# Attention and longformer MLP: the order of a batch's attention inside the MLP groups, and the slots of loads, transposes and copies

## The chip, the cores and the metric

The kernel runs on one core of a Trainium2 chip. A core has a matrix engine (PE, TensorE), three engines for elementwise work (DVE or VectorE, ACT or ScalarE, POOL or GpSimd) and a queue that issues transfers (SP, SyncE). Each takes its instructions in the order in which they stand. The metric is the device time of one execution in microseconds; smaller is better.

## The reference

Eight batches of eight heads of attention over 576 positions of 64 values. A position sees those at most 32 away; eight global positions see all and are seen by all. The heads are put side by side (512 values a position) and go through a residual MLP that mixes the positions first and then the channels.

```
mask = np.abs(pos[:, None] - pos[None, :]) <= window
mask = mask | is_global[:, None] | is_global[None, :]
scores = np.where(mask, scale * np.matmul(q, k.transpose(0, 1, 3, 2)), -1000000000.0)
x = softmax(scores) @ v
...
a1 = alpha1 * x + beta1
u = x + lam * np.einsum('ts,bsd->btd', w_tok, a1)
a2 = alpha2 * u + beta2
out = u + lam * (np.maximum(a2 @ w_ch1, 0.0) @ w_ch2)
```

## The kernel before

**Attention of a batch.** Heads are taken in four pairs (hp). For a pair, `sc_unit` (three of them, u = 0, 1, 2) multiplies QP (the queries, padded and with the global queries behind each block) by KT into one of two PSUM banks, and ACT writes the exponentials E. After the third unit DVE makes PGQ (the global queries' share, L295) and PT (the masked band, L300). `gk_half` gives the scores of all queries against the global keys (EG, then G on DVE). `gq_pv` multiplies PGQ by V; ACT and then DVE (L315, L316) make RG of it, one of two buffers. `pv_x` and `pv_y` (five tiles, `pv_mms`) add G x RG and PT x V; DVE takes the reciprocal (L341) and norms into XR or SR (L348), and POOL multiplies by lambda alpha into XL (L366, L392, L396). The products of `gq_pv`, `pv_x`, `pv_y` and the token mix share a ring of three banks.

**Token mix.** `tok_tile` multiplies XL by the token weights; DVE adds it to XR (L405); POOL scales it into UB, one of two buffers (L420); SP issues a transposing transfer into UT (L421). UT, one of two buffers, is the MLP's input.

**MLP.** The 36 row tiles are taken in nine groups of four (GROUPS). A group is 128 matmuls of 128x512: 64 for the first layer (ACT's ReLU into HT, L488) and 64 for the second, whose result DVE scales and adds (L503, L504) and SP writes out (L507, L509). Group 1 takes the four tiles of batch 1; group 2 a shared tile of the batches 0 and 1 and the first three of batch 2; the later groups need fewer tiles of the batch just mixed.

**What sets the order.** All of it is written out by hand. The loop runs over the groups g = 0 to 8; the 128 matmuls are slots 0 to 127. `weave` spreads a list of atoms (a weight and a function) over a range of slots, in proportion to the weights: those of the attention of batch g + 1 (`attention`, or `first_attention` for batch 1 in group 0) and of its token mix. `timed` spreads by count: for batch g + 2 the loads on POOL (`prefetch`: K and Q in five chunks each, then V in five), on SP the transposes of K and Q into KT and QT (`xbars`) and a copy of V (`copy_vo`), and on DVE the copies from QT to QP (`qpad`, L210, eight of them) and of the global columns (`gcols`, L216 and L222). QP and QT have one buffer each; KT, V and its copy have two.

Of the kernel before, what the change touches and what calls it, by code (L numbers as in the profile page):

```python
# [20 lines left out]
HP = 4  # L21
# [65 lines left out]
def kernel(ctx, tc, q, k, v, global_idx, alpha1, beta1, w_tok, alpha2, beta2, w_ch1, w_ch2, lam, out):  # L87
# [160 lines left out]
    def gk_half(b, hf):  # L248
        def f():
            ps = sc_ps()  # L250
            qs = slice(288 * hf, 288 * hf + 288)
            for hp in range(HP):
                mm(ps[:, 0:288], KGP[:, hp, :], QT[:, hp, qs], hp == 0, hp == HP - 1)
            nc.scalar.activation(out=EG[:, qs], in_=ps[:, 0:288], func=AF.Exp, bias=0.0, scale=0.125)
            if hf == 1:
                g_rows()

        return (1.0, f)
# [14 lines left out]
    def sc_unit(b, hp, u):  # L273
        def f():
            ps = sc_ps()
            e = E[hp % 2]
            off = 0
            for t in (3 * u, 3 * u + 1, 3 * u + 2):
                n = 72 if t % 2 == 0 else 64
                mm(  # L280
                    ps[:, off : off + 2 * n].rearrange("p (a j) -> p a j", a=2),
                    KT[b % 2][:, hp, 64 * t : 64 * t + P],
                    QP[:, hp, :, t, 0:n],
                    True,
                    True,
                )
                off += 2 * n
            nc.scalar.activation(out=e[:, UOFF[u] : UOFF[u + 1]], in_=ps[:, 0:off], func=AF.Exp, bias=0.0, scale=0.125)  # L288
            if u == 2:
                pt, pg = PT[hp % 2], PGQ[hp]  # L290
                p0, p1 = pt.ap[0], e.ap[0]
                gq_in = bass.AP(e.tensor, e.offset + 64, [p1, [272, 5], [72, 2], [1, 8]])
                gq_m = bass.AP(gqm.tensor, gqm.offset, [gqm.ap[0], [8, 5], [0, 2], [1, 8]])
                for c0 in (64, 96):
                    nc.vector.tensor_tensor(  # L295
                        out=pg[:, :, c0 : c0 + 16].rearrange("p c (a g) -> p c a g", a=2), in0=gq_in, in1=gq_m, op=ALU.mult
                    )
                for par, n in ((0, 5), (1, 4)):
                    w = 72 if par == 0 else 64
                    nc.vector.tensor_tensor(  # L300
                        out=bass.AP(pt.tensor, pt.offset + 64 + 128 * par, [p0, [256, n], [1216, 2], [1, 64]]),
                        in0=bass.AP(e.tensor, e.offset + 144 * par, [p1, [272, n], [w, 2], [1, 64]]),
                        in1=bass.AP(mask.tensor, mask.offset + 64 * par, [mask.ap[0], [128, n], [0, 2], [1, 64]]),
                        op=ALU.mult,
                    )

        return (0.6, f)

    def gq_pv(b, hp):
        def f():  # L310
            ps = pv_ps()
            for c in range(5):
                mm(ps[:, 0:130], PGQ[hp][:, c, :], Ve[b % 2][:, c, 2 * hp : 2 * hp + 2, :].rearrange("p a e -> p (a e)"), c == 0, c == 4)
            rg = RG[hp % 2]
            nc.scalar.activation(out=rg, in_=ps[:, 0:130], func=AF.Copy, bias=0.0, scale=C32[:, 36:37])  # L315
            nc.vector.scalar_tensor_tensor(  # L316
                out=rg[96:128], in0=ps[96:128, 0:130], scalar=1.0 / GSC, in1=rg[96:128], op0=ALU.mult, op1=ALU.subtract
            )

        return (0.9, f)  # L320
# [29 lines left out]
    def xl_eng(b):  # L350
        return nc.gpsimd

    def pv_x(b, hp):
        st = {}

        def tile_i(i):
            def f():
                if i == 0:
                    st["ps"] = pv_ps()
                pv_mms(b, hp, i, st["ps"][:, 130 * i : 130 * i + 130])  # L360
                if i == 2:
                    base = 4 * (b % 3)
                    xo = XR[:, base : base + 3, 128 * hp : 128 * hp + 128]
                    norm(st["ps"], recip(st["ps"], 3), 0, 3, 0, P, xo.rearrange("p i (a d) -> p i a d", a=2))
                    l = LA1[:, 128 * hp : 128 * hp + 128]
                    xl_eng(b).tensor_tensor(  # L366
                        out=XL[b % 2][:, 0:3, 128 * hp : 128 * hp + 128],
                        in0=xo,
                        in1=bass.AP(l.tensor, l.offset, [l.ap[0], [0, 3], [1, 128]]),
                        op=ALU.mult,  # L370
                    )

            return (0.75, f)

        return [tile_i(i) for i in range(3)]

    def pv_y(b, hp):
        st = {}
        par = b % 2
        cs = slice(128 * hp, 128 * hp + 128)  # L380

        def f3():
            st["ps"] = pv_ps()
            pv_mms(b, hp, 3, st["ps"][:, 0:130])

        def f4():
            ps = st["ps"]
            pv_mms(b, hp, 4, ps[:, 130:260])
            xo = XR[:, 4 * (b % 3) + 3, cs]
            rt = recip(ps, 2)  # L390
            norm(ps, rt, 0, 1, 0, P, xo.rearrange("p (i a d) -> p i a d", i=1, a=2))
            xl_eng(b).tensor_tensor(out=XL[par][:, 3, cs], in0=xo, in1=LA1[:, cs], op=ALU.mult)  # L392
            r0 = 64 * par
            xo = SR[r0 : r0 + 64, (b // 2) % 2, cs]
            norm(ps, rt, 1, 1, r0, r0 + 64, xo.rearrange("p (i a d) -> p i a d", i=1, a=2))
            xl_eng(b).tensor_tensor(out=XL4[par][r0 : r0 + 64, cs], in0=xo, in1=LA1[r0 : r0 + 64, cs], op=ALU.mult)  # L396

        return [(0.75, f3), (0.4, f4)]
# [37 lines left out]
    def tok_shared(p):  # L436
# [15 lines left out]

        return [half(0), half(1)]

    def attention(b):
        a = []
        for i in range(HP + 1):
            s = [sc_unit(b, i, u) for u in range(3)] if i < HP else []
            w = pv_x(b, i - 1) + pv_y(b, i - 1) if i > 0 else []
            if i == 0:  # L460
                a += s + [gk_half(b, 0), gk_half(b, 1)]
            elif not s:
                a += w
            else:
                a += [s[0], s[1], w[0], w[1], w[2], s[2], w[3], w[4]]
            if i < HP:
                a.append(gq_pv(b, i))
        return a

    def token_mix(b):  # L470
        a = [tok_tile(b, i) for i in range(4)]
# [108 lines left out]
    def first_attention(b):  # L580

        pss = [None, None]

        def hold():
            pss[0], pss[1] = pv_ps(), pv_ps()

        def s(hp):
            return [sc_unit(b, hp, u) for u in range(3)]

        tail = s(0) + [gk_pair(0, pss)] + s(1) + [gk_pair(1, pss), gk_pair(2, pss), gk_pair(3, pss), gq_pv(b, 0)]  # L590
        if b == 0:
            a = [tr_pair(b, hp) for hp in range(HP)] + [(0.0, lambda: gcols(b)), (0.0, hold)] + tail
        else:
            a = [tr_pair(b, 0), (0.0, lambda: gcols(b)), (0.0, hold), tr_pair(b, 1)] + tail[0:4] + [tr_pair(b, 2)] + tail[4:8] + [tr_pair(b, 3)] + tail[8:]
        for hp in range(HP):
            s3 = s(hp + 2) if hp + 2 < HP else []
            g1 = [gq_pv(b, hp + 1)] if hp + 1 < HP else []
            a += s3[0:2] + pv_x(b, hp) + pv_y(b, hp) + g1 + s3[2:3]
        return a

    VF = [t.bitcast(FP32) for t in Vef]
# [230 lines left out]
    for g in range(9):  # L832
        base = mlp(g)
        slots = [[] for _ in range(129)]
        nb = g + 2
        if nb < NB:
            if nb % 2 == 0:
                pr = nb // 2
                slots[1].append(lambda pr=pr: gather(pr))
                slots[44] += [lambda: gather_x(0), lambda: gather_x(1)]  # L840
                slots[56].append(lambda pr=pr: gather_tr(pr, 0))
                slots[60].append(lambda pr=pr: gather_tr(pr, 1))
            timed(prefetch(nb), slots, 2, 60)
            timed(xbars(nb), slots, 60, 100)
            timed([lambda hp=hp: qpad(hp) for hp in range(HP)] + [lambda: gcols(nb)], slots, 116, 127)

        def wrap(i):
            def f():
                for s in slots[i]:
                    s()  # L850
                base[i]()

            return f

        items = [wrap(i) for i in range(128)]
        if g == 0:
            parts = [(first_attention(1), 4, 112), (token_mix(1), 112, 124)]
        elif g + 1 < NB:
            parts = [(attention(g + 1), 2, 90), (token_mix(g + 1), 94, 114)]
        else:  # L860
            parts = []
        weave(items, parts)
# [30 lines left out]
```

## Time and profile before

| | us |
|---|---|
| median of three runs | 435.84 |
| lowest and highest of them | 433.72, 438.39 |
| the profiled execution's own time | 438.8 |
| its span, first to last instruction | 437.0 |
| first matmul of the groups 0 to 8 | 55.3, 109.7, 152.1, 197.3, 240.3, 285.6, 328.6, 376.0, 403.6 |
| granted clock of PE, mean | 0.981 |

A row of the timeline gives the start and the length in us, the engine, the line in the code, the operation, the tile written and the tiles read, and in brackets how long the engine had been idle and what ended that. Rows of equal instructions are merged (x8). PEld is PE's weight load, SPq the queue of SP. A line of waits gives total, number and longest. A matmul's shown end is modelled.

### The profile page before, as it was taken

What the parts mean: (1) busy time and instruction counts of PE and PEld (TensorE: products, weight loads), DVE (VectorE), ACT (ScalarE), POOL (GpSimd) and SP (SyncE); (2) the same over time, 40 slices, a digit from 0 to 9 for tenths busy, and PEclk for the clock granted to TensorE, in tenths of its full rate; (3) what the DMA queues carried; (4) which work ended last, traced back from release to release, by engine and by line L of the source; (5) the groups of instructions that cost most, each with busy time, mean ns of one, the idle gap of its engine ahead of it and who ended that gap; (6) DMA issues with size and microseconds to landing.
All of it is one profiled execution on the core that took longest, in us unless ns stands there. A gap on an engine that the chain in (4) does not pass through costs nothing.

```text
span 437.0 us, 7829 instructions
## 1 busy us (share of the span) xinstructions
PE 383.1 (88%) x2925; PEld 210.3 (48%) x2977; DVE 236.4 (54%) x616; ACT 169.1 (39%) x315; POOL 212.0 (49%) x272
## 2 busy tenths in 40 slices
PE   2385799888999989998999899979997999999994
PEld 1264455543555455544554465445544554444442
DVE  4787464567355746655557565664566365304022
ACT  3563057400681078006820681057304830360720
POOL 8845962435693479347844793377441225100000
PEclk9999889999899999999999999999998999999998
DMA  8999999153994599469966994799673003201002
GB/s 205 206 218 251 221 181 141 11 145 74 126 127 69 133 147 147 57 137 137 141 68 146 138 146 65 125 134 150 67 149 64 1 1 84 72 1 72 26 24 73
DMA packets 162858, 48.97 MB, mean 112 GB/s; under 512 B 147642, under 2 KB 156674, under 8 KB 162820
## 3 DMA queue, kind: packets, MB, share of 16 engines
q0 software_dynamic: 98848, 16.92, 56.1%
q1 hardware_dynamic: 63172, 31.15, 34.5%
q8 instruction: 23, 0.38, 0.4%
q10 hardware_dynamic: 800, 0.39, 0.4%
q14 instruction: 15, 0.12, 0.1%
HBM read 39.34 MB, written 9.44 MB: 112 GB/s over the span
## 4 chain that ended last, share of the span: by engine, by line
PE 67%; DVE 14%; DMA 8%; issue 4%; POOL 4%; ACT 2%; SPq 0%; DVEq 0%; ACTq 0%; POOLq 0%
PE bank L114 67%; DMA Ve<-in_v_dram 7%; DVE QP L210 4%; ACT E L288 2%; DVE PGQ L295 1%; DVE OT L503 1%; DMA UT<-UB 1%; DVE PT L300 1%; DVE QP L567 1%; DVE XR L348 1%; DVE XR L405 1%; DVE SR L348 1%; POOL UB L420 1%; DVE RG L316 1%; DVE KGP L216 1%
## 5 line engine op out<-in xcount | busy, mean ns | idle before, releaser
L114 PE MATMUL bank<-UT,W 128*128 128x512 bf16 x550 | 154.3, 386 | 3.4 <-DMA UT<-UB 2.2
L114 PE MATMUL bank<-W,HT 128*128 128x512 bf16 x553 | 140.0, 379 | 1.0
L488 ACT ACTIVATE HT<-bank,bias 128x512 bf16<-128x512 f32 x144 | 98.8, 686 | 67.8 <-PE bank L114 63.6
L288 ACT ACTIVATE E<-bank 128x416 f16<-128x416 f32 (+1 forms) x96 | 47.1, 511 | 135.6 <-PE bank L114 135.0
L114 PEld LDWEIGHTS <-HT 128*128 128x128 bf16 x576 | 51.4, 97 | 48.7 <-issue 0.3
L366 POOL TENSOR_TENSOR XL<-XR,LA 128x384 bf16<-128x384 f32 x32 | 31.8, 995 | 85.3 <-DVE XR L348 52.5
L114 PEld LDWEIGHTS <-W 128*128 128x128 bf16 x640 | 51.1, 99 | 29.9 <-issue 3.9
L420 POOL TENSOR_TENSOR UB<-XR,A 128x512 bf16<-128x512 f32 x28 | 35.5, 1269 | 46.2 <-DMA UT<-UB 25.0
L114 PE MATMUL bank<-RG,G 128*128 128x65 f16 x320 | 43.0, 192 | 10.4 <-DVE RG L316 10.3
L503 DVE TENSOR_TENSOR OT<-bank,LAM 128x512 f32<-128x512 f32 x36 | 24.7, 685 | 50.1 <-PE bank L114 50.0
L114 PE MATMUL bank<-XL,wtT 128*128 128x512 bf16 x180 | 46.6, 388 | 3.8 <-POOL XL L366 3.7
L114 PEld LDWEIGHTS <-PT 128*128 128x128 f16 x576 | 32.6, 98 | 28.3 <-issue 12.7
L114 PE MATMUL bank<-QP,KT 128*128 128x144 bf16 (+1 forms) x288 | 34.4, 234 | 13.1 <-DVE QP L222 10.3
L114 PE MATMUL bank<-Ve,PT 128*128 128x65 f16 x320 | 43.1, 194 | 0.0
L114 PEld LDWEIGHTS <-KT 128*128 128x128 bf16 x288 | 25.5, 103 | 35.6 <-issue 14.7
L341 DVE RECIPROCAL rd<-bank 128x6 f32<-128x6 f32 x64 | 11.8, 184 | 52.1 <-PE bank L114 52.0
L114 PEld LDWEIGHTS <-G 128*128 128x128 f16 x320 | 30.7, 97 | 16.9 <-DVE G L244 0.3
L405 DVE TENSOR_TENSOR XR<-bank,XR 128x512 f32<-128x512 f32 x32 | 22.0, 688 | 30.4 <-PE bank L114 27.7
L194 POOL DMA_DIRECT2D Ve<-in_v_dram x40 | 34.5, 873 | 2.1 <-DMA HT<-in_moe_w_tok_dram 1.2
L114 PE MATMUL bank<-Vo,PT 128*128 128x65 f16 x256 | 34.9, 192 | 0.0
L295 DVE TENSOR_TENSOR PGQ<-E,gqm 128x80 f16<-128x80 f16 x64 | 16.2, 293 | 28.4 <-ACT E L288 28.4
L114 PEld LDWEIGHTS <-wtT 128*128 128x128 bf16 x180 | 17.9, 99 | 25.5 <-issue 4.8
(117 smaller groups left out, 413.5 us busy)
## 6 DMA issues: line engine op xcount, KB each, us to landing
out_dram<-XR SPq DMA_DIRECT2D x32, 256.0 KB, 2.2
Vo<-Ve SPq DMA_DIRECT2D x16, 260.0 KB, 3.9
W<-in_moe_w_ch_dram POOLq DMA_DIRECT2D x8, 512.0 KB, 18.2
Ve<-in_v_dram POOLq DMA_DIRECT2D x24, 128.0 KB, 5.3
Kb<-in_k_dram POOLq DMA_DIRECT2D x24, 128.0 KB, 6.2
Qb<-in_q_dram POOLq DMA_DIRECT2D x24, 128.0 KB, 6.0
XR<-in_k_dram SPq DMA_DIRECT2D x3, 512.0 KB, 8.2
XR<-in_q_dram SPq DMA_DIRECT2D x3, 512.0 KB, 9.3
```

Source lines behind the costliest of these rows:

```text
L114: nc.tensor.matmul(out=o, lhsT=l, rhs=r, start=st, stop=sp, skip_group_check=True)
L194: nc.gpsimd.dma_start(out=Ve[b % 2][r0 : r0 + hi - lo, c, :, 0:D], in_=v[b, :, lo:hi, :].rearrange("h p d -> p h d"))
L210: nc.vector.tensor_copy(out=QP[r, hp, a, :, 0:64], in_=QT[r, hp, 0:S].rearrange("p (t j) -> p t j", j=64))
L288: nc.scalar.activation(out=e[:, UOFF[u] : UOFF[u + 1]], in_=ps[:, 0:off], func=AF.Exp, bias=0.0, scale=0.125)
L295: nc.vector.tensor_tensor(out=pg[:, :, c0 : c0 + 16].rearrange("p c (a g) -> p c a g", a=2), in0=gq_in, in1=gq_m, op=ALU.mult)
L341: nc.vector.reciprocal(out=rt[:, 0 : 2 * n], in_=ps[:, 0 : 130 * n].rearrange("p (i e) -> p i e", e=65)[:, :, 64:65].rearrange("p i o -> p ...
L348: nc.vector.tensor_tensor(out=xo, in0=pv[:, :, :, 0:64], in1=rb, op=ALU.mult)
L366: xl_eng(b).tensor_tensor(out=XL[b % 2][:, 0:3, 128 * hp : 128 * hp + 128], in0=xo, in1=bass.AP(l.tensor, l.offset, [l.ap[0], [0, 3], [1, ...
L405: nc.vector.tensor_tensor(out=x, in0=ps, in1=x, op=ALU.add)
L420: nc.gpsimd.tensor_tensor(out=ub, in0=x, in1=A2, op=ALU.mult)
L488: nc.scalar.activation(out=HT[:, ec, :], in_=st["ps"], func=AF.Relu, bias=bias1[:, ec : ec + 1], scale=1.0)
L503: nc.vector.tensor_tensor(out=ot, in0=ps, in1=LAM, op=ALU.mult)
```

## The change

The attention of the batches 2 to 7 is put in another order. The first pair's units get gaps (weights without an instruction) between them, so that MLP matmuls fall there. From the second pair on the list is: first score unit, `gq_pv` of the pair before, the other two units, a gap, then PV of the pair before. Behind PV of pair 2 stand a gap, `gq_pv` of pair 3, a gap and PV of pair 3. In group 0 the product of pair 3 goes ahead of PV of pair 2, with a gap behind it and one ahead. The ranges of slots change: the attention ends earlier, the token mix begins later (in group 0 earlier), loads, transposes and copies go earlier.

```diff
+    def gap(w):
+        return (w, lambda: None)
+
     def attention(b):
         a = []
-        for i in range(HP + 1):
-            s = [sc_unit(b, i, u) for u in range(3)] if i < HP else []
-            w = pv_x(b, i - 1) + pv_y(b, i - 1) if i > 0 else []
+        for i in range(HP):
+            s = [sc_unit(b, i, u) for u in range(3)]
             if i == 0:
-                a += s + [gk_half(b, 0), gk_half(b, 1)]
-            elif not s:
-                a += w
+                a += [s[0], s[1], gap(0.6), s[2], gap(0.6), gk_half(b, 0), gap(0.8), gk_half(b, 1), gap(0.4)]
             else:
-                a += [s[0], s[1], w[0], w[1], w[2], s[2], w[3], w[4]]
-            if i < HP:
-                a.append(gq_pv(b, i))
-        return a
+                a += [s[0], gq_pv(b, i - 1), s[1], s[2], gap(0.3)] + pv_x(b, i - 1) + pv_y(b, i - 1)
+        return a + [gap(0.3), gq_pv(b, HP - 1), gap(1.2)] + pv_x(b, HP - 1) + pv_y(b, HP - 1)
...
-            a += s3[0:2] + pv_x(b, hp) + pv_y(b, hp) + g1 + s3[2:3]
+            if b == 1 and hp == 2:
+                a += g1 + [gap(1.2)] + pv_x(b, hp) + pv_y(b, hp)
+            else:
+                a += s3[0:2] + pv_x(b, hp) + pv_y(b, hp) + g1 + s3[2:3] + ([gap(1.0)] if b == 1 and hp == 1 else [])
...
-            timed(prefetch(nb), slots, 2, 60)
-            timed(xbars(nb), slots, 60, 100)
-            timed([lambda hp=hp: qpad(hp) for hp in range(HP)] + [lambda: gcols(nb)], slots, 116, 127)
+            timed(prefetch(nb), slots, 1, 50)
+            timed(xbars(nb), slots, 44, 78)
+            timed([lambda hp=hp: qpad(hp) for hp in range(HP)] + [lambda: gcols(nb)], slots, 86, 104)
...
-            parts = [(first_attention(1), 4, 112), (token_mix(1), 112, 124)]
+            parts = [(first_attention(1), 4, 98), (token_mix(1), 106, 120)]
         elif g + 1 < NB:
-            parts = [(attention(g + 1), 2, 90), (token_mix(g + 1), 94, 114)]
+            parts = [(attention(g + 1), 2, 83), (token_mix(g + 1), 97, 115 if g < 3 else 122)]
```

What this makes of the order on the engines, at three places. In the changed kernel the lines behind `attention` stand two lower in number at first (L503 is L501), and one higher at the end.

DVE in group 2, the last pair of batch 3; RG_96 is that pair's RG, PT_90 its band, bank_68 the bank of PV's last two tiles of the pair before. Before:

```order
L295 TENSOR_TENSOR PGQ_94<-E_88,gqm 128x5x16 x2
L300 TENSOR_TENSOR PT_90<-E_88,mask 128x5x2x64
L300 TENSOR_TENSOR PT_90<-E_88,mask 128x4x2x64
L341 RECIPROCAL rd_101<-bank_68 128x4
L348 TENSOR_TENSOR XR<-bank_68,rd_101 128x128
L348 TENSOR_TENSOR SR<-bank_68,rd_101 64x128
L316 SCALAR_TENSOR_TENSOR RG_96<-bank_69,RG_96 32x130
```

And now, from the same PT on (L237 writes the global columns of a later batch):

```order
L300 TENSOR_TENSOR PT_90<-E_88,mask 128x4x2x64
L237 CAST KGT<-bank_68 128x128
L237 CAST QGT<-bank_70 128x128
L341 RECIPROCAL rd_100<-bank_69 128x6
L348 TENSOR_TENSOR XR<-bank_69,rd_100 128x3x128
L341 RECIPROCAL rd_101<-bank_68 128x4
L348 TENSOR_TENSOR XR<-bank_68,rd_101 128x128
L348 TENSOR_TENSOR SR<-bank_68,rd_101 64x128
L316 SCALAR_TENSOR_TENSOR RG_96<-bank_69,RG_96 32x130
```

PT and PGQ of the last pair now stand a whole PV of the pair before ahead of its RG; only that PV's last norms are left directly in front.

DVE at the end of group 2, from the token mix on; the last row is already group 3's. Before:

```order
L405 TENSOR_TENSOR XR<-bank_69,XR 128x512
L405 TENSOR_TENSOR SR<-bank_70,SR 128x512
L503 TENSOR_TENSOR OT<-bank_64,LAM 128x512
L504 TENSOR_TENSOR XR<-OT,XR 128x512
L210 COPY QP<-QT 64x9x64 x8
L216 COPY KGP<-KGT 128x4x16
L222 COPY QP<-QGT 128x4x5x8 x2
L503 TENSOR_TENSOR OT<-bank_65,LAM 128x512
L504 TENSOR_TENSOR XR<-OT,XR 128x512
L295 TENSOR_TENSOR PGQ_91<-E_87,gqm 128x5x16 x2
```

And now, from the last norm of the attention to the last two tiles of the mix:

```order
L348 TENSOR_TENSOR SR<-bank_68,rd_103 64x128
L210 COPY QP<-QT 64x9x64 x6
L501 TENSOR_TENSOR OT<-bank_63,LAM 128x512
L502 TENSOR_TENSOR XR<-OT,XR 128x512
L210 COPY QP<-QT 64x9x64 x2
L405 TENSOR_TENSOR XR<-bank_69,XR 128x512
L405 TENSOR_TENSOR XR<-bank_70,XR 128x512
L216 COPY KGP<-KGT 128x4x16
L222 COPY QP<-QGT 128x4x5x8 x2
L405 TENSOR_TENSOR XR<-bank_68,XR 128x512
L405 TENSOR_TENSOR XR<-bank_69,XR 128x512
```

The copies into QP moved from behind the whole token mix to ahead of its first L405.

SP in group 3, around its first output (L509, now L507). Before:

```order
L205 DMA_TRANSPOSE QT<-Qb 128x4x128
L509 DMA out_dram<-XR 128x512
L202 DMA_TRANSPOSE KT_80<-Kb 128x4x128
L205 DMA_TRANSPOSE QT<-Qb 128x4x128
L202 DMA_TRANSPOSE KT_80<-Kb 128x4x128
L205 DMA_TRANSPOSE QT<-Qb 128x4x128
L421 DMA_TRANSPOSE UT_112<-UB_110 128x4x128
```

And now:

```order
L202 DMA_TRANSPOSE KT_80<-Kb 128x4x128
L205 DMA_TRANSPOSE QT<-Qb 128x4x128
L198 DMA Vo_86<-Ve_84 64x2080
L199 DMA Vo_86<-Ve_84 64x2080
L507 DMA out_dram<-XR 128x512 x2
L421 DMA_TRANSPOSE UT_112<-UB_110 128x4x128
```

The transposes of K and Q and the copy of V no longer stand behind an output of the group.

## The prediction

> **What bounds the kernel now.** I read the page's busy shares first, then who waited for whom on PE, then the timeline at the places that this names, and last the granted clock there. Group g means pass g of the loop over nine MLP groups, and b = g + 1 the batch whose attention is woven into it.
>
> Page, part 1, and PE's waits: the first list is 109 to 376 us (groups 1 to 6), the second 55 to 109.8 (group 0); us in total, times, longest.
>
> ```profile
> PE 383.1 (88%) x2925; PEld 210.3 (48%) x2977; DVE 236.4 (54%) x616; ACT 169.1 (39%) x315; POOL 212.0 (49%) x272
> ...
> PE bank L114 <- DVE QP L222: 9.6, 5, 2.7
> PE bank L114 <- DVE RG L316: 3.8, 6, 0.7
> PE bank L114 <- DMA UT<-UB: 2.2, 1, 2.2
> PE bank L114 <- ACT E L288: 1.0, 4, 0.4
> PE bank L114 <- DVE PGQ L295: 0.2, 1, 0.2
> ...
> PE bank L114 <- DVE RG L316: 2.3, 2, 1.3
> PE bank L114 <- DMA UT<-UB: 2.2, 1, 2.2
> PE bank L114 <- DVE QP L567: 1.5, 2, 0.8
> ...
> PEld L114 <- DVE PGQ L295: 4.6, 18, 0.3
> ```
>
> PE is busy for 88% and no other engine passes 54%. So the span is PE's own work plus what it waits for, and the lists name nearly all the waits after 55 us. (The 2.2 of UT is one wait, at 109.74, in both lists.) Next, three places in the timeline: start, length, engine, line, tiles.
>
> ```profile
> 194.71 2.75 PE L114 MATMUL bank<-W,HT 128*128 128x512 bf16 x12
> 195.62 3.66 DVE L210 COPY QP<-QT 64x576 bf16<-64x576 bf16 x8
> 197.30 0.59 PE L114 MATMUL bank<-UT,W 128*128 128x512 bf16 x2
> 199.39 0.30 DVE L222 COPY QP<-QGT 128x160 bf16<-128x160 bf16 x2
> 199.75 0.34 PE L114 MATMUL bank<-QP,KT 128*128 128x144 bf16 x3 [1.85 <-DVE QP L222]
> ```
>
> Group 3 starts at 197.30; two MLP matmuls later PE needs QP, whose eight copies have just run. The first row gives PE's step: (2.75 - 0.38) / 11 = 0.215 us a matmul, although each shows 0.38. So an idle gap costs 0.16 more than it shows, and one slot of the 128-slot list is 0.215 us of MLP.
>
> ```profile
> 175.46 0.34 PE L114 MATMUL bank<-QP,KT 128*128 128x144 bf16 x3
> 176.45 0.87 DVE L295 TENSOR_TENSOR PGQ<-E,gqm 128x80 f16<-128x80 f16 x2 [0.43 <-ACT E L288]
> 177.03 0.38 PE L114 MATMUL bank<-W,HT 128*128 128x512 bf16 x1
> 177.38 0.46 PE L114 MATMUL bank<-Ve,PGQ 128*128 128x130 f16 x5
> 177.24 0.81 DVE L300 TENSOR_TENSOR PT<-E,mask 128x640 f16<-128x640 f16 x2
> 178.50 0.29 DVE L348 TENSOR_TENSOR SR<-bank,rd 64x128 f32<-64x128 f32 x1
> 178.83 0.30 DVE L316 SCALAR_TENSOR_TENSOR RG<-bank,RG 32x130 f16<-32x130 f32 x1
> 179.18 0.19 PE L114 MATMUL bank<-RG,G 128*128 128x65 f16 x1 [0.70 <-DVE RG L316]
> ```
>
> The last pair of batch 3: the global-query product starts at 177.38, its result RG passes DVE behind PT and the norms, and PV starts 1.80 later with three matmuls between.
>
> ```profile
> 98.93 0.68 DVE L405 TENSOR_TENSOR XR<-bank,XR 128x512 f32<-128x512 f32 x1
> 104.59 2.49 POOL L420 TENSOR_TENSOR UB<-XR,A 128x512 bf16<-128x512 f32 x2 [2.27 <-DMA UT<-UB]
> 109.74 0.88 PE L114 MATMUL bank<-UT,W 128*128 128x512 bf16 x2 [2.16 <-DMA UT<-UB]
> ...
> 109.90:113.30 3.40, 3.40 (x16) 1.91 (x15) 0.36 (x1) 1.60 (x3) 3.40 (x5) 0.50 0.95 88
> 288.11 0.34 PE L114 MATMUL bank<-QP,KT 128*128 128x144 bf16 x3 [1.94 <-DVE QP L222]
> 288.20:291.60 3.40, 2.98 (x23) 1.85 (x24) 2.18 (x6) 2.72 (x6) 3.40 (x5) 1.00 1.33 161
> 331.88 0.38 PE L114 MATMUL bank<-QP,KT 128*128 128x144 bf16 x2 [2.66 <-DVE QP L222]
> 331.90:335.10 3.20, 3.20 (x15) 1.80 (x15) 1.21 (x2) 1.84 (x4) 0.00 (x0) 0.50 0.58 182
> ```
>
> The end of group 0: four token-mix tiles go DVE L405, POOL L420 (two UB buffers), transposing DMA; 10.8 us from the first L405 to the next group's first matmul. The rows that begin with A:B are stretches of time, with PE's busy time after the length and the granted clock third from the end: 0.50 after that wait of 2.16 and after the longest QP wait, 2.66, but 1.00 after the one of 1.94.
>
> **The change part by part: what goes.** No instruction is added or removed; gaps are weights in the weave. Every item is a place where an instruction waits now.
>
> QP copies and gcols move from slots 116-127 to 86-104, so QP is done some 20 slots before the next group's slot 2: 9.6 + 5 x 0.16 = 10.4. The clock: each half-speed stretch loses half of PE's 3.40 and 3.20, together 3.3, if no idle gap over 1.94 is left. The last pair gets gap(0.3), gq_pv, gap(1.2): attention weights now sum to 31.2 over slots 2-83 (2.60 slots a unit; before 26.4 over 2-90, 3.33), so 0.9 + 1.2 = 2.1 units put six matmuls between product and PV, 6 x 0.215 + 0.29 = 1.58; and PT is no longer ahead of RG on DVE, which takes the 0.81 out of the 1.80. It fits: 3.8 + 6 x 0.16 = 4.8 goes. Spaced first units: 1.0 + 4 x 0.16 = 1.6. PGQ is now made a whole PV ahead of its use; each of the 18 weight-load waits costs PE only what it shows beyond the step (177.03 to 177.38 is 0.35, so 0.13), a few nothing, one 0.35: about 2.0. Group 0: PV of pairs 2 and 3 gets the gaps and pair 3's product before pair 2's PV: 2.3 + 2 x 0.16 = 2.6. Its token mix starts at slot 106, not 112, which gives the UT wait (2.16 + 0.16 = 2.3) room. Sum of what can go: 10.4 + 3.3 + 4.8 + 1.6 + 2.0 + 2.6 + 2.3 = 27.0.
>
> **What comes.** Group 0 is packed tighter (slots 4-98, 2.78 a unit, before 3.42). Two QP L567 waits grow by 1.2 x 0.64 = 0.77 slot, 0.17 each: 0.3. Pair 3's product now follows its third score unit after five matmuls, 5 x 0.215 + 0.19 = 1.27, and score to PGQ takes 177.32 - 175.46 = 1.86: 0.6. Between slots 86 and 106 DVE has the eight copies (3.7), an output (1.4) and 3 us of norms, against PE's 20 x 0.215 + 1.3 = 5.6: the token mix waits some 0.6 more for XL. UT: from the first tile's end to the group's end PE now has 22 slots and 25 matmuls, 10.1; needed are 0.3 + 10.7, so 0.9 stays at worst, 0 if the first transpose isn't held up; I take 0.5. Together 2.0, between 0.3 (the transposes alone) and 2.4.
>
> Group 1 needs its third tile (slot 106, before 104). On DVE the copies (3.7), an output (1.4) and a norm (0.7) stand ahead of its first L405, 5.8 us against PE's 3.8. So the chain starts 2.0 late, and UT lands 0.6 to 1.8 after PE asks; nothing hides it. I take 0.8. Groups 2 to 6 have 1.6 us or more of room, since their next group needs only the first to third of their tiles, and the longer span to slot 122 moves only later ones.
>
> Pairs 0 to 2: product, two score units, gap, PV: 6 x 0.215 + 0.29 + 0.37 = 1.95 now, 2.15 before. The chain from product to RG is 1.75 in the rows above (177.38 to 179.13), with PT ahead of it; in the new order it is ScalarE's exponential of the first unit that stands ahead. So 0 by that row; the other end is group 0's worst wait, 1.3 + 0.16 less its shorter distance, say 0.65 a pair, 12 in all. The place is nearest to the first row; I take 0.15 for 18 pairs, 2.7.
>
> Loads go to slots 1-50, transposes to 44-78. On SP they leave their place behind the first output of the group:
>
> ```profile
> 211.59 1.72 SPq L205 DMA_TRANSPOSE QT<-Qb  x1
> 226.55 0.34 SPq L509 DMA_DIRECT2D out_dram<-XR  x1
> 230.93 1.22 SPq L205 DMA_TRANSPOSE QT<-Qb  x1
> ...
> 212.53 0.72 POOL L187 DMA_DIRECT2D Qb<-in_q_dram  x1
> Qb<-in_q_dram POOLq DMA_DIRECT2D x24, 128.0 KB, 6.0
> ```
>
> The last Q chunk was issued at 212.53 and lands about 6.0 later, 21 us into group 3; its transpose ran at 230.93 only because the output at 226.55 was ahead. Now it can run by 25 us, and slot 86 is 86 x 0.215 + 8.6 of attention = 27 us in. POOL (49% busy) takes the loads earlier and its XL later, which nobody asks for before slot 97. Cost nothing; if that cover goes, see the third rival.
>
> Sum: 27.0 - 2.0 - 0.8 - 2.7 = 21.5. Against this execution (span 437.0, time 438.8) that is a span of 415.5; its time is 3.0 above the median of the three runs, so I take the difference from the median: 435.8 - 21.5 = 414.3.
>
> [...] In the new slots POOL's XL and UB run beside the copies. Eight copies take 3.66 at 195.62, and four take 1.82 in the first row here while UB (104.59 to 107.08) runs: 0.46 each in both.
>
> ```profile
> 103.98 1.82 DVE L210 COPY QP<-QT 64x576 bf16<-64x576 bf16 x4
> L366 POOL TENSOR_TENSOR XL<-XR,LA 128x384 bf16<-128x384 f32 x32 | 31.8, 995 | 85.3 <-DVE XR L348 52.5
> ```
>
> [...]
>
> **Rivals.** (1) RG stays late in pairs 0 to 2, because ScalarE is full there: 12 instead of 2.7, 423.6. For: the distance shrinks by 0.2. Against: no wait there now, with 1.75 for the chain. (2) The QP wait gives way to UT at the ends of groups 0, 1 and 2, each 2.3 with 1.7 of half clock, 12.0 instead of 1.3: 425.0. For: group 0 does this today, and copies now stand ahead of L405. Against: room of 1.6 in group 2, and the clock held after 1.94. (3) Slower: the copies reach DVE's queue before QT has landed. DVE is in order, so L405 and the norms stand behind them and PE stops at the fourth tile (slot 110, 33 us in). If QT came as late as now (230.93 + 3, 37 us in), with copies and L405 that is 8 us a group in six groups: 414.3 + 48 = 462. It decides from about 32.6 us in, where the loss is 3.6 a group. Against: nothing is left ahead of the transposes on SP. [...] (5) The change doesn't act: not possible for the order, which is written out by hand.
>
> **Chances.** My case 0.70 (409 to 420), rival 1 0.10, rival 2 0.12, rival 4 0.02, rival 3 0.06, half of it within 1%. About 1% is what a measurement of this kernel can tell from no change. So faster 0.94, same 0.03, slower 0.03. The range goes from all 27.0 with nothing new, 408.8, with 1 off for the spread of the runs, to rival 2's 425.0 with 1 on it: 408 to 426.
>
> **What would show it.** PE's waits without QP L222; RG L316 under 1.5 in total after group 0; granted clock 1.00 from 60 us to the end's last slice; QT's transposes ahead of the output on SP; a UT wait of about 0.8 at group 2's start. Wrong if a UT or RG row above 5 us appears, or if DVE shows L210 waiting for a DMA.

## The result, and the profile after

The changed kernel takes 421.9 us, the median of four executions (419.3 to 425.7), beside 437.1 for the kernel before on the same chip: a ratio of 0.966 with a 95% interval of 0.956 to 0.976, 15 us less. The forecast was 414.3 within 408 to 426, faster with 0.94. So the sign and the range held, and the middle was 7.6 us too low. The profiled execution of the new kernel, at 419.3, is the fastest of its four; its span is 19.5 us below that of the profiled execution before (437.0 - 417.5). Two more profiles of the same kernel, taken with the experiments, have spans of 422.2 and 423.1. All ratios are of executions in the faster of two states; of the ten executions of `copies_alone` one took 812.6 us, for a cause that no trace shows, and stands outside its ratio.

Where the 19.5 sits is seen from the first matmul of each group (`bank<-UT,W` in the timeline; us, the first column is what the prologue took):

| profiled execution | start of group 0 | group 0 | groups 1 to 6 | groups 7, 8 | span |
|---|---|---|---|---|---|
| before | 55.3 | 54.4 | 266.3 | 61.1 | 437.0 |
| changed, first | 54.1 | 53.8 | 248.5 | 61.1 | 417.5 |
| changed, second | 56.2 | 54.5 | 250.4 | 61.1 | 422.2 |
| changed, third | 57.2 | 54.5 | 250.3 | 61.1 | 423.1 |

The change works in groups 1 to 6 (16 to 18 us) and hardly in group 0, where 2.9 was forecast. Part of the 16 to 18 is the clock. PE runs at half clock in stretches of 3.4 us (granted 0.50 in the profile before from 109.91 and from 331.78 us), and by their length each costs 1.7 where PE is busy. Groups 1 to 6 hold these two in the profile before, none in the first profile of the changed kernel (granted 1.00 from 60 to 410 us) and one in its second and third. `group0_alone` (below), which leaves groups 1 to 6 as they were, has none there and takes 262.7. With 1.7 taken off for each stretch, all three profiles of the changed kernel lose about 14.2. The start of group 0 is code that the change doesn't touch; over all profiles of this study it lies between 54.1 and 58.9, and the first profile of the changed kernel had the earliest.

The page of the changed kernel, busy time and shares, and the granted clock of its 40 slices:

```profile
PE 377.9 (91%) x2977; PEld 208.3 (50%) x2977; DVE 235.9 (56%) x616; ACT 166.4 (40%) x315; POOL 212.7 (51%) x272
...
PEclk9999889999999999999999999999999999999999
```

PE now stands at 91%, and no slice from 63 us on (the seventh and later) is below 0.9 of full clock. The next list is what PE waited for from 53 us to the end, in the same kernel: us in total, times, longest.

```profile
PE bank L114 <- DMA UT<-UB: 4.6, 3, 2.3
PE bank L114 <- DVE QP L565: 2.0, 3, 1.0
PE bank L114 <- POOL XL L392: 1.1, 1, 1.1
PE bank L114 <- DVE KGT L237: 1.0, 2, 0.7
PE bank L114 <- DVE XR L348: 0.4, 1, 0.4
PE bank L114 <- POOL XL L396: 0.2, 1, 0.2
```

The rows of QP L222 (9.6), RG (3.8 and 2.3), E (1.0) and PGQ have gone altogether. What was one UT wait of 2.2 is now three, 4.6 together; KGT is new, and XL stands at 1.3 where it was 0.2. The timeline at the start of group 3, the place of the second fence of the prediction:

```profile
191.29 0.59 PE L114 MATMUL bank<-UT,W 128*128 128x512 bf16 x2
191.72 0.34 PE L114 MATMUL bank<-QP,KT 128*128 128x144 bf16 x3
```

QP is read 0.43 after the group's first matmul, with no bracket behind the row: nothing is waited for, where 1.85 was. And the last pair of batch 3, in group 2 (the third fence of the prediction):

```profile
170.72 0.45 PE L114 MATMUL bank<-Ve,PGQ 128*128 128x130 f16 x5
171.03 0.29 DVE L348 TENSOR_TENSOR SR<-bank,rd 64x128 f32<-64x128 f32 x1
171.25 0.37 ACT L315 ACTIVATE RG<-bank,C 128x130 f16<-128x130 f32 x1 [1.27 <-PE bank L114]
171.66 0.30 DVE L316 SCALAR_TENSOR_TENSOR RG<-bank,RG 32x130 f16<-32x130 f32 x1 [0.33 <-ACT RG L315]
172.30 0.19 PE L114 MATMUL bank<-RG,G 128*128 128x65 f16 x1
```

From the product to PV are 1.58 us (172.30 - 170.72), the very figure worked out, and RG is done 0.34 before PV, since DVE now waits for it (the 0.33 in brackets) and not it for DVE. On SP in group 3 the last transposes stand ahead of the output, as forecast:

```profile
210.19 2.17 SPq L202 DMA_TRANSPOSE KT<-Kb  x1
212.45 1.23 SPq L205 DMA_TRANSPOSE QT<-Qb  x1
...
219.61 4.84 SPq L507 DMA_DIRECT2D out_dram<-XR  x2
```

What did not go is the wait at the end of group 0. Timeline of the changed kernel there, SP's transposes, POOL's conversions into the two UB buffers and the next group's first matmul:

```profile
95.69 0.69 DVE L405 TENSOR_TENSOR XR<-bank,XR 128x512 f32<-128x512 f32 x1
96.52 2.55 POOL L420 TENSOR_TENSOR UB<-XR,A 128x512 bf16<-128x512 f32 x2 [1.46 <-issue]
101.73 2.50 POOL L420 TENSOR_TENSOR UB<-XR,A 128x512 bf16<-128x512 f32 x2 [2.66 <-DMA UT<-UB]
103.03 1.19 SPq L421 DMA_TRANSPOSE UT<-UB  x1
104.75 0.34 SPq L507 DMA_DIRECT2D out_dram<-XR  x1
105.20 1.23 SPq L421 DMA_TRANSPOSE UT<-UB  x1
107.90 0.59 PE L114 MATMUL bank<-UT,W 128*128 128x512 bf16 x2 [2.27 <-DMA UT<-UB]
```

From the first L405 to the matmul are 12.21 us; PE ran out of other work after 9.94 (107.90 - 2.27 - 95.69). The third UB waits until the first is transposed (POOL idle 2.66), and the fourth UB, ready at 104.23, is not sent until 105.20, because an output stands ahead of it on SP.

### The profile page after: what moved, and what is told of

Its sections match the earlier page's. It is cut to its first block, busy times and chain, and to the rows that moved or that the text cites. A ratio compares the mean times of both kernels' runs of the same rounds, so it can differ in the third digit from the quotient of the medians.

```text
span 417.5 us, 7876 instructions
## 1 busy us (share of the span) xinstructions
PE 377.9 (91%) x2977; PEld 208.3 (50%) x2977; DVE 235.9 (56%) x616; ACT 166.4 (40%) x315; POOL 212.7 (51%) x272
## 4 chain that ended last, share of the span: by engine, by line
PE 65%; DMA 12%; DVE 10%; POOL 6%; issue 2%; ACT 2%; SPq 1%; DVEq 0%; POOLq 0%
PE bank L114 65%; DMA Ve<-in_v_dram 7%; DMA UT<-UB 3%; DVE QP L210 2%; DMA QT<-Qb 2%; POOL UB L420 1%; DVE QP L565 1%; POOL KQG L226 1%; DVE OT L501 1%; ACT HT L486 1%; DVE XR L502 1%; SPq L202 1%; ACT E L288 1%; DVE PT L300 1%; DVE QP L222 1%
## 5 line engine op out<-in xcount | busy, mean ns | idle before, releaser
L114 PE MATMUL bank<-UT,W 128*128 128x512 bf16 x576 | 160.7, 380 | 4.6 <-DMA UT<-UB 4.6
L114 PEld LDWEIGHTS <-HT 128*128 128x128 bf16 x576 | 52.9, 98 | 54.5 <-issue 0.4
L501 DVE TENSOR_TENSOR OT<-bank,LAM 128x512 f32<-128x512 f32 x36 | 24.8, 688 | 56.0 <-PE bank L114 55.8
L114 PE MATMUL bank<-QP,KT 128*128 128x144 bf16 (+1 forms) x288 | 33.0, 228 | 3.5 <-DVE QP L565 1.7
L114 PEld LDWEIGHTS <-KT 128*128 128x128 bf16 x288 | 24.6, 100 | 21.8 <-issue 3.8
L295 DVE TENSOR_TENSOR PGQ<-E,gqm 128x80 f16<-128x80 f16 x64 | 11.5, 220 | 37.4 <-ACT E L288 34.8
L405 DVE TENSOR_TENSOR XR<-bank,XR 128x512 f32<-128x512 f32 x32 | 21.5, 685 | 13.8 <-PE bank L114 13.3
L348 DVE TENSOR_TENSOR XR<-bank,rd 128x384 f32<-128x384 f32 x64 | 27.1, 424 | 2.3
```

The source lines that it names most:

```text
L114: nc.tensor.matmul(out=o, lhsT=l, rhs=r, start=st, stop=sp, skip_group_check=True)
L295: nc.vector.tensor_tensor(out=pg[:, :, c0 : c0 + 16].rearrange("p c (a g) -> p c a g", a=2), in0=gq_in, in1=gq_m, op=ALU.mult)
L348: nc.vector.tensor_tensor(out=xo, in0=pv[:, :, :, 0:64], in1=rb, op=ALU.mult)
L405: nc.vector.tensor_tensor(out=x, in0=ps, in1=x, op=ALU.add)
L501: nc.vector.tensor_tensor(out=ot, in0=ps, in1=LAM, op=ALU.mult)
```

## The experiments

All ratios are to the kernel before, measured beside each. The first four kernels are the kernel before with one part of the change put in; the others are the changed kernel, again or with an edit. `copies_alone`, `attention_alone` and `group0_alone` together are the whole change, apart from the ranges of attention and token mix in groups 1 to 6.

**Loads, transposes and copies alone** (`copies_alone`).

```diff
-            timed(prefetch(nb), slots, 2, 60)
-            timed(xbars(nb), slots, 60, 100)
-            timed([lambda hp=hp: qpad(hp) for hp in range(HP)] + [lambda: gcols(nb)], slots, 116, 127)
+            timed(prefetch(nb), slots, 1, 50)
+            timed(xbars(nb), slots, 44, 78)
+            timed([lambda hp=hp: qpad(hp) for hp in range(HP)] + [lambda: gcols(nb)], slots, 86, 104)
```

> The kernel before with the three new slot ranges alone: loads 1 to 50, transposes 44 to 78, copies into QP 86 to 104. Own theory (each wait stands for itself): the five QP waits go, 9.6 + 5 x 0.16 = 10.4 us, and the half clock behind the longest, 1.6; the copies ahead of the first L405 cost about 1 us of UT wait at the start of group 2; so 11 us less than before, and the RG waits of the last pairs (3.8 us over groups 1 to 6) stay. Rival (the tail takes over): the QP wait hid the UT chain, UT waits of 1 to 2 us come at the starts of groups 2 to 6 with half clock behind some, and no more than 4 us are gained.

436.8 us, ratio 0.990 (0.985 to 0.994). QP L222 is gone, and groups 1 to 6 take 258.2, 8.1 less. UT did not take over (2.8 in all). But group 0 grew by 5.3. The timeline of this kernel there:

```profile
95.72 0.69 DVE L504 TENSOR_TENSOR XR<-OT,XR 128x512 f32<-128x512 f32 x1
96.33 0.90 DVE L210 COPY QP<-QT 64x576 bf16<-64x576 bf16 x2
97.26 0.30 DVE L316 SCALAR_TENSOR_TENSOR RG<-bank,RG 32x130 f16<-32x130 f32 x1
97.61 0.21 PE L114 MATMUL bank<-RG,G 128*128 128x65 f16 x1 [3.39 <-DVE RG L316]
```

In group 0 the old attention still runs to slot 112, so the copies meet it: two of them stand directly ahead of RG, PE waits 3.39, and the clock is at half (granted 0.50) for 6.8 us from 96.3. So the total agrees with the smaller of the two expectations, but not for its reason.

**The same with group 0 as it was** (`copies_from_group1`).

```diff
-            timed(prefetch(nb), slots, 2, 60)
+            timed(prefetch(nb), slots, *((1, 50) if g > 0 else (2, 60)))
...
-            timed([lambda hp=hp: qpad(hp) for hp in range(HP)] + [lambda: gcols(nb)], slots, 116, 127)
+            timed([lambda hp=hp: qpad(hp) for hp in range(HP)] + [lambda: gcols(nb)], slots, *((86, 104) if g > 0 else (116, 127)))
```

(the transposes likewise)

> The kernel before with the three new slot ranges from group 1 on; group 0 keeps the old ones. In the run with the new ranges everywhere, group 0 became 5.3 us longer (a wait for RG of 3.4 where copies into QP stood ahead of it on DVE, and half clock behind that), and groups 1 to 6 together 8.1 shorter. Theory: the copies cost group 0 only because its attention ends at slot 112, behind them. Then group 0 is back at 54 to 55 us, groups 1 to 6 stay at 257 to 260, and 8 to 10 us are gained. Rival: the loss in group 0 came from the earlier loads and transposes; groups 1 to 6 then pay for theirs too, and no more than 5 us are gained.

432.3 us, 0.980 (0.973 to 0.987). Groups 1 to 6 take 258.2 again, and group 0 54.6. The waits of PE from 53 us on in this kernel:

```profile
PE bank L114 <- DVE RG L316: 6.1, 8, 1.3
PE bank L114 <- DMA UT<-UB: 2.6, 2, 2.4
PE bank L114 <- DVE PGQ L295: 2.0, 5, 0.6
```

So the early copies are worth about 8 us where they don't meet the attention of group 0. They leave RG where it was (6.1 before too), but PE's waits for PGQ rise from 0.2 to 2.0. One stretch at half clock is left in groups 1 to 6, where the profile before has two, so 1.7 of the 8 is the clock.

**The order inside the attention alone** (`attention_alone`): `attention(b)` and `gap` as in the diff of the change, all ranges as before.

```diff
+    def gap(w):
+        return (w, lambda: None)
...
-                a += [s[0], s[1], w[0], w[1], w[2], s[2], w[3], w[4]]
-            if i < HP:
-                a.append(gq_pv(b, i))
-        return a
+                a += [s[0], gq_pv(b, i - 1), s[1], s[2], gap(0.3)] + pv_x(b, i - 1) + pv_y(b, i - 1)
+        return a + [gap(0.3), gq_pv(b, HP - 1), gap(1.2)] + pv_x(b, HP - 1) + pv_y(b, HP - 1)
```

> The kernel before with the new attention list of the batches 2 to 7 alone, in the old slot ranges. Own theory: the waits for RG (3.8 + 6 x 0.16 = 4.8), for the score banks (1.6) and for PGQ (2.0) go, 8.4 us less than before, and the five QP waits (9.6) stay. Rival: PE reaches the group's end earlier while the copies on DVE come no earlier, so what is gained within a group comes back as a longer QP wait: QP L222 near 15 us, and 2 to 3 us gained in all.

430.2 us, 0.978 (0.971 to 0.984). Its waits:

```profile
PE bank L114 <- DVE QP L222: 9.9, 5, 2.4
PE bank L114 <- DVE RG L316: 2.3, 2, 1.3
PE bank L114 <- DMA UT<-UB: 2.2, 1, 2.2
```

E and PGQ are gone, RG stays in group 0 alone, and QP is what it was. Groups 1 to 6 lose 7.9 (266.3 to 258.4), near the 8.4 expected, and both stretches at half clock are still there. The two parts add up: with 1.7 off for each stretch, the early copies take 6.3 and the order 7.9, 14.2 together, which is what the changed kernel loses. So the ranges of attention and token mix in groups 1 to 6, which were not tried by themselves, have, by this sum, next to nothing left to explain.

**Group 0 alone** (`group0_alone`).

```diff
+            if b == 1 and hp == 2:
+                a += g1 + [gap(1.2)] + pv_x(b, hp) + pv_y(b, hp)
+            else:
+                a += s3[0:2] + pv_x(b, hp) + pv_y(b, hp) + g1 + s3[2:3] + ([gap(1.0)] if b == 1 and hp == 1 else [])
...
-            parts = [(first_attention(1), 4, 112), (token_mix(1), 112, 124)]
+            parts = [(first_attention(1), 4, 98), (token_mix(1), 106, 120)]
```

> The kernel before with group 0's part alone: the new order of pairs 2 and 3 of batch 1, its attention in slots 4 to 98 and its token mix in 106 to 120. In the changed kernel group 0 gained only 0.6 us (54.42 to 53.81). Theory A (the copies into QP, which in the full change stand ahead of group 0's first L405, ate the gain): without them here group 0 takes 49.5 to 51 us and the UT wait at group 1's start is under 1. Theory B (the chain of two UB buffers and transposes sets the end whatever stands ahead): the UT wait stays at 2 or more, group 0 takes 52.5 to 54.

437.0 us, 0.995 (0.992 to 0.998); group 0 53.4, 1.1 less. RG of group 0 is gone, yet the UT wait at its end is 2.52, although here no early copy stands ahead of the token mix. So an earlier slot for the mix doesn't buy the wait off, and the copies are not what keeps it. Left as a cause is the chain through the two UB buffers, with the output that stands ahead of the fourth transpose here too (0.98 between UB and its transpose).

**The changed kernel again** (`after_again`, `after_third`), with no edit, in two sets.

> The changed kernel once more, as the measure for the others of this job: 0.966 of the time before, 419 to 424 us. If the parts add up, the three kernels of this job together save what this one saves, about 15 to 19 us; if the parts stand in each other's way they save clearly more or less.

> The changed kernel again, as the measure for this job: 0.966 of the time before, half clock after the UT wait at the start of group 1 in some executions and not in others.

424.0 us, 0.966 (0.959 to 0.974), and 425.3, 0.968 (0.963 to 0.972). The UT waits are 4.8 and 5.3 in all, the longest 2.6 in both. Behind it a stretch at half clock is seen, which the first profile lacks. Windows of 3.4 us behind that wait, clock third from the end; the first profile, then the second:

```profile
107.90:111.30 3.40, 3.40 (x25) 2.00 (x26) 0.66 (x4) 2.59 (x6) 3.40 (x5) 1.00 1.31 161
```

```profile
111.10:114.50 3.40, 3.40 (x16) 1.90 (x15) 0.00 (x0) 1.87 (x4) 3.40 (x5) 0.50 1.47 176
```

25 matmuls against 16 in the same time; group 1 takes 42.6 instead of 40.95. By the ratios `copies_alone`, `attention_alone` and `group0_alone` save 4.6, 9.9 and 2.4 us, 16.9 together, beside 14.8 here; with intervals as wide as these that is no difference. The first profile, on which one would have judged the change, was a lucky one by this 1.7 and by 2.1 to 3.1 in the prologue.

**The gaps without weight** (`no_gaps`).

```diff
-        return (w, lambda: None)
+        return (0.0 * w, lambda: None)
```

> The changed kernel with all gap weights at zero, same order of the atoms, same ranges. Theory: the order alone does not do it, the gaps do: the last pair's product and PV stand 0.9 units = 2.8 slots apart (0.6 + 0.29 us) against a chain of 1.2 to 1.75, so RG waits of 0.3 to 0.8 come back in seven groups, and score bank waits of 0.2 to 0.4 in six: 4 to 8 us slower than the changed kernel. Rival: the order does it, since PT is no longer ahead of RG on DVE: under 2 us slower.

425.4 us, 0.963 (0.957 to 0.969): no different from the changed kernel. Small RG waits come back, 0.14 to 0.19 in each of groups 1 to 6, and one PGQ wait of 0.5; E stays away. On the other side KGT's waits leave PE's list. Groups 1 to 6 take 250.7, beside 250.3 and 250.4. So the new order does the work, and what the gaps add can't be measured.

**The transposes later** (`transposes_mid`), in slots 60 to 86, and the loads in 2 to 60 (rival 3 of the prediction, in small).

```diff
-            timed(prefetch(nb), slots, 1, 50)
-            timed(xbars(nb), slots, 44, 78)
+            timed(prefetch(nb), slots, 2, 60)
+            timed(xbars(nb), slots, 60, 86)
```

> The changed kernel with loads in slots 2 to 60 and transposes in 60 to 86, so that the last transpose of Q stands at slot 81 behind the group's first output, and the copies into QP still at 86. Theory (the prediction's third rival, in small): DVE reaches the copies before QT has landed, stands 2 to 4 us in each of six groups, and the first L405 with it; at the ends of groups 0, 1 and 3 PE sees it: 4 to 9 us slower than the changed kernel, DVE's wait of L210 for a DMA above 10 us in all (1.7 now). Rival: the cover is wide, under 1 us.

436.2 us, 0.993 (0.988 to 0.998): nearly the whole gain is lost, 12 us, more than the 4 to 9 expected. What DVE waited for ahead of QP's copies, from the view of tile QP, and PE's waits:

```profile
  DMA QT<-Qb: 10.9, 4
```

```profile
PE bank L114 <- DVE XR L405: 5.7, 4, 2.5
PE bank L114 <- DMA UT<-UB: 5.5, 2, 3.1
PE bank L114 <- POOL XL L366: 2.1, 1, 2.1
```

The copies wait 10.9 for QT (1.7 in the changed kernel), L405 stands behind them on DVE, and PE waits for L405's bank, then for XL and UT. Copies at slot 86 need transposes that are early: the two moves are one. (The loads went back with the transposes; how much is theirs was not tried.)

**Three UB buffers** (`ub3`).

```diff
-    UB = [T(f"UB{i}", [P, DM], BF16) for i in range(2)]
+    UB = [T(f"UB{i}", [P, DM], BF16) for i in range(3)]
...
-        ub = UB[nub[0] % 2]
+        ub = UB[nub[0] % 3]
```

> The changed kernel with three UB buffers in place of two. The UT waits (4.6 to 4.8 us at the starts of groups 1, 2 and 4, and half clock behind the first in some runs) are what is left. Theory A: with two buffers the third tile waits until the first's transpose has landed (POOL idle 2.7 there); with three that wait goes, UT waits fall to under 2 us, 2 to 5 us faster than the changed kernel. Theory B: the transposes themselves follow each other no faster than one in 2 us (the first takes 3.9 where a second is issued 1.3 behind it, 2.6 where 2.1 behind); a third buffer changes nothing, the UT waits stay over 4.

417.8 us, 0.945 (0.939 to 0.952), below the interval of the changed kernel. Group 0 takes 51.6, 2.2 to 2.9 less. Timeline at its end:

```profile
100.09 0.69 DVE L405 TENSOR_TENSOR XR<-bank,XR 128x512 f32<-128x512 f32 x1
103.71 1.27 POOL L420 TENSOR_TENSOR UB<-XR,A 128x512 bf16<-128x512 f32 x1 [0.24 <-DVE XR L405]
106.26 1.27 POOL L420 TENSOR_TENSOR UB<-XR,A 128x512 bf16<-128x512 f32 x1 [1.28 <-DVE XR L405]
106.97 0.34 SPq L507 DMA_DIRECT2D out_dram<-XR  x1
107.56 3.50 SPq L421 DMA_TRANSPOSE UT<-UB  x2
110.11 0.59 PE L114 MATMUL bank<-UT,W 128*128 128x512 bf16 x2
```

The third UB now waits for its own data alone, the output on SP is past before the fourth UB is ready (107.53), the chain is 10.02 instead of 12.21, and PE doesn't wait. So with a third buffer the wait is gone. The output's hold on SP went with it, so this run doesn't tell how the two shared the 12.21.

**Copies of group 0 later** (`g0_copies_later`), and **the global columns ahead of the copies** (`gcols_first`), one profiled execution each.

```diff
-            timed([lambda hp=hp: qpad(hp) for hp in range(HP)] + [lambda: gcols(nb)], slots, 86, 104)
+            timed([lambda hp=hp: qpad(hp) for hp in range(HP)] + [lambda: gcols(nb)], slots, *((107, 121) if g == 0 else (86, 104)))
```

> The changed kernel with the copies of group 0 alone in slots 107 to 121, behind its first L405. Theory: they delay the last pair's norm there, so the token mix's wait for XL (1.1 + 0.2) goes and its first L405 comes 1.1 earlier; but the two UB buffers still pace what follows, so the UT wait stays at 2 to 2.6, and group 0 takes 52.5 to 53.5 (53.8 and 54.5 in the changed kernel). Rival: the copies are what holds up the tail, and the UT wait falls under 1.

421.8 us. The XL wait of 1.1 is gone, so the copies ahead of the norms did make it; group 0 takes 53.0. The UT wait remains, 2.79: with two buffers the early copies are not what makes it.

```diff
-            timed([lambda hp=hp: qpad(hp) for hp in range(HP)] + [lambda: gcols(nb)], slots, 86, 104)
+            timed([lambda: gcols(nb)] + [lambda hp=hp: qpad(hp) for hp in range(HP)], slots, 84, 100)
```

> The changed kernel with the global columns ahead of the QP copies, in slots 84 to 100, two UB buffers. In the changed kernel the second L222 takes 1.30 us instead of 0.19 in two groups, while a UB operation of POOL runs, and the second L405 behind it comes 1.1 late. Theory A (DVE copy and POOL exclude each other): no L222 above 0.25, and the UT wait at the start of group 4 (1.1) goes. Theory B: the long L222 is its own wait for data; it stays at 1.3 wherever it stands.

427.7 us. In groups 1 to 6 the longest L222 falls from 1.30 to 0.45 us, which is neither theory's figure, and UT's waits don't go: 2.36 at group 1's start, 2.06 at group 2's (1.19 before this edit), 0.87 at group 4's (1.13). By this one execution the long copy (last section) is not what makes UT late, save perhaps for 0.3 in group 4.

**Everything together** (`combined`): three UB buffers, the global columns first (slots 84 to 100, in group 0 99 to 116), and the transposes of gathered columns in slots 70 and 72 instead of 56 and 60 from group 1 on.

```diff
+    UB = [T(f"UB{i}", [P, DM], BF16) for i in range(3)]
...
+        ub = UB[nub[0] % 3]
...
+                slots[56 if g == 0 else 70].append(lambda pr=pr: gather_tr(pr, 0))
+                slots[60 if g == 0 else 72].append(lambda pr=pr: gather_tr(pr, 1))
...
+            timed([lambda: gcols(nb)] + [lambda hp=hp: qpad(hp) for hp in range(HP)], slots, *((99, 116) if g == 0 else (84, 100)))
```

> The changed kernel with three UB buffers, the global columns ahead of the QP copies (slots 84 to 100, in group 0 99 to 116) and the transposes of gathered columns at slots 70 and 72 from group 1 on. Theory: the waits left in the run with three buffers go: UT at the starts of groups 2 and 4 (0.7 and 0.9), KGT in groups 2 and 4 (0.8), XL in group 0 (1.2): 3 to 4 us under that run, 0.94 of the time before. Rival: PE asks sooner, but the transposes set the ends now; UT waits of 1.5 or more remain, and it equals the run with three buffers (0.945).

419.1 us, 0.952 (0.948 to 0.956). KGT and XL are gone from the list, but UT is at 2.8 (1.5 of it at group 1's start), and L405's bank takes 0.9 in group 2. At group 1's start DVE reaches the fourth L405 only at 105.48, behind an addition for the output and two of the copies, so UT comes late there in spite of the third buffer. This kernel and the one with three buffers alone can't be told apart: their intervals overlap.

## Why the prediction came out as it did

**What held.** The 22.1 us forecast for groups 1 to 6 (10.4 of QP, 3.3 of clock, 4.8 of the last pair's RG, 1.6 of E, 2.0 of PGQ) went in the first profile, less what came there; in the second and third half of the 3.3 of clock stayed. `copies_from_group1` and `attention_alone` show that each part takes away its own waits; the early copies alone also brought waits for PGQ (2.0 instead of 0.2), which the new order doesn't have. In group 0 RG's 2.6 went. The transposes on SP stand where the prediction put them, and `transposes_mid` shows that its third rival was a real one: later loads and transposes cost 12 us. UT at group 2's start was taken at 0.8 and is 1.19 (1.35 with the 0.16 of each gap). QP L565, taken at 0.3 more, went from 1.5 to 2.0.

**What was too dear.** RG in pairs 0 to 2 was taken at 2.7 and is 0, without the gaps too: the waits under 0.2 that come back in `no_gaps` are the last pair's. PGQ in group 0 was taken at 0.6; PE doesn't wait for it, one weight load does, for 0.4.

**What failed: the step "needed are 0.3 + 10.7".** The prediction gave PE 10.1 us of work from the first tile's end to the group's end, and took the chain of the UB buffers at its length in the kernel before. PE's part came out at 9.94. The chain became 12.21: the first transpose landed later (POOL's idle time 2.66, before 2.27), and an output now stands on SP between the third and fourth transposes, with 0.97 between the fourth UB's end and its transpose; in the kernel before the five transposes were one run from 101.04. These are 0.4 and 1.0 of the 1.4 by which the chain grew. The runs divide at the second: with the token mix in slots 112 to 124 (`copies_from_group1`, `attention_alone`) no output stands there and the chain takes 11.0 and 10.9; with it in 106 to 120 (`group0_alone`, `g0_copies_later`) the output holds the fourth transpose for 1.0 and the chain takes 12.6 and 12.9. So the earlier slot itself put the transpose behind the output. The term of 2.3 "room" was therefore nothing (2.27 against 2.16), and the sum was 1.8 too high by it (2.3 less the 0.5 kept). In the second and third profile half clock came back with it, 1.7. That a third buffer takes the wait away is shown by `ub3`, and that the early copies don't make it by `group0_alone` and `g0_copies_later`; how much the output on SP costs by itself was not tried, since `ub3` removes both. Why the first transpose landed later is open.

**What was not seen.** Group 4 starts with a UT wait of 1.13, where the prediction saw "1.6 us or more of room" in groups 2 to 6. And the transposes of gathered columns take two of three banks that PV uses; in the timeline of the changed kernel, group 2:

```profile
169.22 0.29 DVE L237 CAST KGT<-bank 128x128 bf16<-128x128 f32 x1
169.42 0.28 DVE L237 CAST QGT<-bank 128x128 bf16<-128x128 f32 x1
169.56 0.19 PE L114 MATMUL bank<-RG,G 128*128 128x65 f16 x1 [0.30 <-DVE KGT L237]
```

PV waits until the cast has emptied the bank, here 0.30, in group 4 0.67. XL in group 0 cost 1.07 + 0.16, where 0.6 was taken.

**The balance.** Forecast 21.5. By the first profile 19.5, of which 1.2 is the prologue. The rest is 17.8 in groups 1 to 6 (forecast 22.1 - 2.7 - 0.8 = 18.6) and 0.6 in group 0 (2.6 + 2.3 - 2.0 = 2.9). By the medians it is 15, and the second profile shows where the difference goes: 1.9 more in groups 1 to 6, nearly all of it group 1 at half clock, 0.7 in group 0 and 2.1 in the prologue. The second rival (UT takes over) came true in part: 4.6 to 5.3 us of waits where it put 6.9, and one stretch at half clock or none where it put three. The first had no part. Of the rival put at 0.02, the fourth, that the copies and POOL's operations hold each other up, the eight copies into QP show nothing: in the profiles before and after none takes over 0.45, beside POOL's UB or XL either. Four short copies of L222 take 1.26 to 1.30 instead of 0.19 (last section). Two signs that the prediction named for being wrong are there in small. The UT row is 4.6, 4.8 and 5.3 in the three profiles, where 5 was the limit. And DVE's L210 waits for QT's transposes in group 3 and group 5, in the second profile in group 4 too: 1.7 in all in the first, 3.9 and 3.8 in the others. So the cover of 2 us (25 against 27) that the prediction gave those copies was not there. At the ends of groups 4 and 5 PE shows no wait for it, at the end of group 3 its UT wait is 0.99, 1.13 and 1.45 behind copies that waited 0.35, 1.10 and 1.32, so they may add to it; that was not tried.

## What to carry to other kernels

When a wait ends last at one place in each of several groups, move everything that its producer needs along with the producer, and see that nothing on its engine's queue is passed that another wait hangs on: the same move gave 8 us in six groups (1.7 of it the clock), where the waits showed 9.6, and cost 5 in the one where it met the attention. Here a wait on a ring of two buffers wasn't bought off by an earlier start, because the chain through the ring started earlier and became longer (12.21 us, before 10.81); one more buffer took the wait away (10.02 in `ub3`). Take at least two profiles of the changed kernel before you explain a few us: here the first was 5 us below the other two, most of it in the prologue and in one stretch at half clock.

## What the runs showed of the hardware

One kind of short copy on DVE was held up for a whole POOL instruction, and another was not. In the changed kernel, the view of tile QP (durations in ns: least, median, most) and the timeline in group 1:

```profile
L210 DVE COPY QP<-QT x48: 434/448/450, 87.8 to 307.6; 64x576 bf16<-64x576 bf16 x48
...
L222 DVE COPY QP<-QGT x16: 189/195/1301, 20.5 to 308.8; 128x160 bf16<-128x160 bf16 x16
```

```profile
141.04 1.41 DVE L222 COPY QP<-QGT 128x160 bf16<-128x160 bf16 x2
141.12 1.27 POOL L420 TENSOR_TENSOR UB<-XR,A 128x512 bf16<-128x512 f32 x1 [5.05 <-DVE XR L405]
```

L222 ends with POOL's UB (142.45 and 142.39) and takes 1.30 instead of 0.19; none of the 48 copies of L210 passes 0.45. In the kernel before, where 27 of them overlap a UB, they take 0.43 to 0.45 too. There are four such long copies of L222 in the profile of the changed kernel, of 1.26 to 1.30 us; each begins 0.03 to 0.11 behind the start of a UB and ends 0.05 to 0.06 behind its end. The first L222 of the row above begins at 141.04, ahead of the UB at 141.12, and takes 0.19. Why L222 is held there and L210 not, no run shows.

A stretch at half clock doesn't follow from the length of PE's idle gap alone. The granted clock was 0.50 behind gaps of 2.16 and 2.66 us in the profile before and of 2.61 in `after_again`; it was 1.00 behind 1.94 in the profile before, 2.27 in the first profile of the changed kernel and 2.79 in `g0_copies_later`. In the profile before, the stretches begin at 55.30, 109.91 and 331.78 us, 16 and 65 times 3.413 apart, and each of the three is 3.413 long. If steps of this length are laid over that profile from 60 to 410 us, counted from its stretches, PE is busy for 1.25 us in the step ahead of 109.91, for 0.85 in the one ahead of 331.78, and for 1.78 or more in every other. Counted in the same way from the stretch at 54.85 in the first profile of the changed kernel, the least is 1.56 (106.05 to 109.46), and the clock stays at 1.00. The gap of 2.27 there lies across 106.05, where two steps meet, with 0.42 ahead and 1.85 behind; the gap of 2.16 in the profile before lies within one step. So in these two profiles the clock goes with how a gap lies; that this decides it in general is not shown. A matmul's shown end is modelled, so the busy times are approximate.
